# Parting the PSUM ring of stage one: two banks for part-array rounds, two for the first layer

## The chip, the cores and the metric

The kernel runs on one core of a Trainium2 chip. The metric is the device time of one execution in microseconds (us). Before the change it is 1588.79 us, the median of three runs (1582.47 to 1589.11). One execution was profiled, with times, waits and the clock of every engine; the rows below come from it. TensorE is called PE here, VectorE DVE, ScalarE ACT, GpSimd POOL, and SP issues the DMAs.

## The reference

An attention through 32 packed queries for each head is followed by two feed-forward layers. The second of these makes up most of the later half of the kernel; the change lies in everything ahead of it.

```python
def sm_attn(qq, kk, vv):
    s = scale * np.matmul(qq, kk.transpose(0, 1, 3, 2))
    s = s - np.max(s, axis=-1, keepdims=True)
    a = np.exp(s)
    a = a / (np.sum(a, axis=-1, keepdims=True) + 1e-09)
    return np.matmul(a, vv)
p_packed = sm_attn(p, k, v)              # 8 batches, 8 heads, 32 x 64
out = sm_attn(q, p_packed, p_packed)     # 576 x 64 for each head
...
h = x @ w_in                             # first layers: 512 -> 2048 -> 512
g = h * np.cos(h)
x = g @ w_out
h = x @ w2_in
g = h * np.tanh(softplus(h))
return g @ w2_out
```

## The kernel before

**Stage one** does the attention and the first feed-forward layer. Its 4608 tokens are 16 tiles of 288 (two for each batch), and the 2048 hidden channels are 16 groups of 128, so there are 256 steps `n`. The second product of the attention is folded into the layer's weights: `w_unit` multiplies the packed rows `PK` of a batch by `w_in`, and `l1` then multiplies those products (`W1`) by the attention weights `AT` of a token tile. A step has three parts on PE and beside it:

- `l1(n)`: six matmuls of 288 columns (each operand is a high and a low part, three products for each of two halves) into one bank of PSUM.
- the chain `chain_first`, `chain_cos`, `chain_split`, which makes `g = h cos h` of that bank: L793 on ACT, L795 and L796 on DVE, the sine L802 on ACT, the product with `h` L803 on DVE (the last reader of the bank), then the high part L810 on ACT and the low part L813 on POOL.
- `l2(n - 3)`: twelve matmuls of 288 columns, three for each of four banks `acc`.

Between these, `run_bg` and `run_ew` bring the background work of the step, planned in the tables `bg_pe`, `bg_ew` and `bg_ld`. Its PE part consists of small rounds in which a matmul fills only a part of the array (64 rows or 128 by 32 columns), so that several of them can run side by side on different parts:

- `k_unit` (16 of them): `s2_pe` scores packed queries against keys, eight matmuls into two banks (L215); `s4_pe` transposes (L250, L251, the whole array); `s5_pe` multiplies by the values, twenty matmuls into one bank (L276); `s6_pe` transposes once more (L294).
- `q_unit` (16): `s2_pe`, eight matmuls into two banks (L348).
- `w_unit` (40): four matmuls for each batch (L488), so eight into two banks where it serves two batches (24 units), four into one bank where it serves one (16 units).

All of these and `l1` take their bank from `ring()`, one ring of four. The other four banks are the accumulators of `l2`. The same `ring` serves the products of stage two. A float32 matmul of such a round leaves two records in the trace, so a round of eight is shown as x16.

The order on each engine is made when the program is built: a scheduler takes the instruction that is ready by its own timeline, by priorities (`tc.high_priority`) and by orders asked for with `tc.issue_after`. In `w_unit` the other matmuls are asked to follow the first; in the other units nothing keeps the matmuls of a round together.

**Stage two** does the second layer in five blocks of tokens, from about 860 us to the end.

Of the kernel before, what the change touches and what calls it, by code (L numbers as in the profile page):

```python
# [8 lines left out]
F32 = mybir.dt.float32  # L9
# [6 lines left out]
B, H, S, D, NPK = 8, 8, 576, 64, 32  # L16
# [52 lines left out]
HP_W = 400  # L69
K3 = (0, 2, 1, 3, 5, 4, 6)  # L70
# [14 lines left out]
def build(tc, q, k, v, p, w1i, w1o, w2i, w2o, out):  # L85
    nc = tc.nc
    ctx = ExitStack()
    with ctx:
# [10 lines left out]
        def ring():  # L99
            return psum.tile([128, 512], F32, tag="ps", bufs=4, name=nm("ps"))  # L100
# [56 lines left out]

        PK = {}
        lastexp = [None]

        def k_unit(b, g, alloc_v):
# [16 lines left out]
            def vload(i):  # L178
                def f():
# [7 lines left out]
                    else:  # L187
                        nc.sync.dma_start(
                            r[:64, :256].rearrange("p (h d) -> p h d", d=D),
# [20 lines left out]
            def s2_pe():  # L210
                st["s1"] = [ring() for _ in range(2)]
                for l in range(4):
                    h = PERM[par][l]
                    for x in range(2):
                        nc.tensor.matmul(  # L215
                            st["s1"][x][32 * l : 32 * l + 32, :TT].rearrange("p (s a) -> p a s", a=9),
                            st["pp"][64 * x : 64 * x + 64, 32 * h : 32 * h + 32],
                            st["kt"][64 * x : 64 * x + 64, TT * h : TT * h + TT].rearrange("p (a s) -> p a s", s=32),
                            start=True,
                            stop=True,  # L220
                        )
# [23 lines left out]
            def s4_pe():  # L245
                e = st["e"]
                t1, t2 = ring(), ring()
                ev = e[:, :512].rearrange("p (t c) -> p c t", c=4)
                for c in range(4):
                    nc.tensor.transpose(t1[:, 128 * c : 128 * c + 128], ev[:, c], ident)  # L250
                nc.tensor.transpose(t2[:64, :128], e[:, 512:576], ident)  # L251
                st["t"] = (t1, t2)

            def s4_ew():
# [4 lines left out]
                nc.scalar.copy(a5[:64], t2[:64, :128])  # L259
# [6 lines left out]
            def s5_pe():  # L266
                a4, a5 = st["a"]
                ps = ring()
                for c in range(5):
                    n = 128 if c < 4 else 64  # L270
                    a = a4[:, 128 * c : 128 * c + 128] if c < 4 else a5[:64]
                    for l in range(4):
                        h = PERM[par][l]
                        vr = st["vr"][h // 2] if c < 4 else st["vr"][2]
                        o = 256 * (h % 2) + D * c if c < 4 else D * h
                        nc.tensor.matmul(  # L276
                            ps[32 * l : 32 * l + 32, :D],
# [200 lines left out]
        def w_unit(bs, fg, g, ms):  # L478
            st = {}

            def pe():
                for b in bs:
                    st[b] = ring()
# [675 lines left out]
```

## Time and profile before

| what | us |
|---|---|
| median of three runs | 1588.79 |
| the profiled execution, its own time | 1587.78 |
| its span, first to last instruction | 1585.8 |
| PE busy in the span | 1492.7 |
| DVE busy | 1093.4 |
| ACT busy | 895.0 |
| POOL busy | 672.3 |

The span is 1.98 us shorter than the execution's own time, and that execution lies 1.01 us under the median. PE is busy for 94% of the span. Matmuls are pipelined and their ends are modelled, so the time that a group of matmuls takes is best read from start to start: when matmuls of 288 columns follow each other without a wait, they start about 0.13 us apart, though each is shown as 0.29 us long.

### The profile page before, as it was taken

How to read it: one execution, taken by the hardware profiler on the slowest of the kernel's cores; microseconds unless marked ns; L12 is line 12 of the kernel's file. 1: busy time of each engine (PE TensorE's matmuls, PEld its weight loads, DVE VectorE, ACT ScalarE, POOL GpSimd, SP SyncE). 2: the span in 40 equal slices, each digit the busy share in tenths (PEclk: the TensorE clock that was granted, in tenths of full speed). 3: DMA queues.
4: the chain of work that ended last, by engine and by line, in shares of the span. 5: the costliest groups of instructions: out<-in, count | busy, mean ns of one | idle time of the engine just before them, and what ended most of it. 6: DMA issues, size and time to landing. Idle time of an engine off the chain costs nothing.

```text
span 1585.8 us, 28624 instructions
## 1 busy us (share of the span) xinstructions
PE 1492.7 (94%) x9728; PEld 1302.5 (82%) x9728; DVE 1093.4 (69%) x2044; ACT 895.0 (56%) x1844; POOL 672.3 (42%) x682
## 2 busy tenths in 40 slices
PE   3778999999999999998999999999999999999997
PEld 1566778788987898788999888889999899999986
DVE  4885667677766776778764557687567658756656
ACT  3675767677766776766764345435444533543343
POOL 0451346357653665647843025225223521532142
PEclk9889999999999999999999999999999999999999
DMA  9888676557556556543323668788778878777955
GB/s 290 276 214 206 175 186 191 170 146 205 154 158 180 168 163 164 175 123 109 120 68 119 198 197 248 204 231 263 232 214 258 253 213 229 240 215 207 262 150 169
DMA packets 250833, 307.05 MB, mean 194 GB/s; under 512 B 104768, under 2 KB 129856, under 8 KB 250688
## 3 DMA queue, kind: packets, MB, share of 16 engines
q1 hardware_dynamic: 250688, 305.22, 66.6%
q8 instruction: 78, 1.28, 0.3%
q14 instruction: 67, 0.55, 0.1%
HBM read 252.71 MB, written 52.43 MB: 192 GB/s over the span
## 4 chain that ended last, share of the span: by engine, by line
PE 70%; DMA 9%; DVE 7%; ACT 4%; issue 4%; POOL 4%; SPq 1%; DVEq 0%; POOLq 0%; ACTq 0%
PE acc L142 12%; PE acc L143 12%; PE acc L144 12%; PE ps L142 10%; PE ps L143 10%; PE ps L144 10%; PE ps L488 2%; POOL wt L563 2%; DMA raw<-in_moe_w_out_dram 2%; DMA raw<-in_moe_w_in_dram 1%; DVE r L796 1%; DMA kr<-in_k_dram 1%; DVE r L795 1%; DMA kr<-in_q_dram 1%; POOL raw L569 1%
## 5 line engine op out<-in xcount | busy, mean ns | idle before, releaser
L813 POOL TENSOR_TENSOR gh<-r,gh 128x288 fp32r<-128x288 f32 x256 | 216.7, 853 | 286.3 <-ACT gh L810 204.1
L937 POOL TENSOR_TENSOR gh<-t,gh 128x448 fp32r<-128x448 f32 (+1 forms) x120 | 155.2, 1298 | 427.9 <-ACT gh L936 427.9
L143 PE MATMUL acc<-gh,wo 128*128 128x288 f32 x1024 | 301.7, 301 | 1.8 <-POOL gh L813 1.6
L144 PE MATMUL acc<-gh,wo 128*128 128x288 f32 x1024 | 298.2, 298 | 0.0
L142 PE MATMUL acc<-gh,wo 128*128 128x288 f32 x1024 | 276.7, 305 | 6.7 <-ACT gh L810 5.9
L142 PEld LDWEIGHTS acc<-gh,wo 128*128 128x128 f32 x1024 | 182.3, 191 | 41.7 <-issue 16.5
L143 PE MATMUL acc<-gh,T 128*128 128x448 f32 (+1 forms) x560 | 209.6, 374 | 1.3 <-DVE gh L937 1.3
L144 PE MATMUL acc<-gh,T 128*128 128x448 f32 (+1 forms) x560 | 208.9, 374 | 0.0
L143 PE MATMUL ps<-wab,ws 128*128 128x448 f32 (+1 forms) x560 | 208.2, 372 | 0.0
L142 PE MATMUL ps<-wab,ws 128*128 128x448 f32 (+1 forms) x560 | 206.7, 372 | 1.3 <-DMA ws<-wst 1.2
L143 PEld LDWEIGHTS acc<-gh,wo 128*128 128x128 f32 x1024 | 194.1, 190 | 15.8 <-issue 10.1
L144 PE MATMUL ps<-wab,ws 128*128 128x448 f32 (+1 forms) x560 | 206.9, 372 | 0.0
L144 PEld LDWEIGHTS acc<-gh,wo 128*128 128x128 f32 x1024 | 194.2, 190 | 4.1 <-issue 4.0
L937 DVE TENSOR_TENSOR gh<-wo,gh 128x448 fp32r<-128x448 f32 (+1 forms) x160 | 128.8, 810 | 95.4 <-ACT gh L936 94.6
L142 PE MATMUL acc<-gh,T 128*128 128x448 f32 (+1 forms) x560 | 186.5, 375 | 3.2 <-ACT gh L936 3.2
L142 PE MATMUL ps<-aT,wab 128*128 128x288 f32 x512 | 161.1, 315 | 28.2 <-DVE r L803 20.1
L802 ACT ACTIVATE r<-r,halfpi 128x288 f32<-128x288 f32 x256 | 136.2, 535 | 84.4 <-DVE r L796 82.8
L803 DVE TENSOR_TENSOR r<-r,ps 128x288 f32<-128x288 f32 x256 | 114.4, 448 | 69.1 <-ACT r L802 68.1
L143 PE MATMUL ps<-aT,wab 128*128 128x288 f32 x512 | 153.1, 299 | 0.0
L144 PE MATMUL ps<-aT,wab 128*128 128x288 f32 x512 | 152.4, 298 | 0.0
L795 DVE SCALAR_TENSOR_TENSOR r<-ki,ps 128x288 f32<-128x288 int32 x256 | 113.5, 446 | 55.0 <-ACT ki L793 35.7
L793 ACT ACTIVATE ki<-ps,quarter 128x288 int32<-128x288 f32 x256 | 124.0, 495 | 47.5 <-PE ps L144 36.8
(150 smaller groups left out, 2968.5 us busy)
## 6 DMA issues: line engine op xcount, KB each, us to landing
ws<-wst SPq DMA_DIRECT2D x280, 256.0 KB, 3.0
T<-tst SPq DMA_DIRECT2D x280, 256.0 KB, 2.9
kr<-in_k_dram SPq DMA_DIRECT2D x64, 272.0 KB, 5.4
ld<-ws SPq DMA_DIRECT2D x64, 256.0 KB, 3.7
kr<-in_q_dram SPq DMA_DIRECT2D x60, 272.0 KB, 5.3
wst<-wt SPq DMA_DIRECT2D x56, 256.0 KB, 2.7
tst<-wt SPq DMA_DIRECT2D x56, 256.0 KB, 2.2
x2d<-xo SPq DMA_DIRECT2D x64, 144.0 KB, 1.8
```

The costliest lines, as they stand in the source:

```text
L142: nc.tensor.matmul(ps, l0, r0, start=first, stop=False, skip_group_check=more)
L143: nc.tensor.matmul(ps, l0, r1, start=False, stop=False, skip_group_check=more)
L144: nc.tensor.matmul(ps, l1, r0, start=False, stop=last, skip_group_check=more)
L488: return nc.tensor.matmul(st[b][32 * l : 32 * l + 32], PK[(b, g)][r : r + 64, 32 * l : 32 * l + 32], ms[h // 2]["m"][r : r + 64], start=Tr ...
L563: nc.gpsimd.tensor_tensor(lo, src, hi, ALU.subtract)
L569: nc.gpsimd.tensor_tensor(quad(raw, a), quad(raw, b), quad(raw, c), d)
L793: nc.scalar.activation(ki, st["h"], AF.Identity, bias=quarter, scale=1.0 / TWO_PI)
L795: nc.vector.scalar_tensor_tensor(r, ki, -TWO_PI, st["h"], ALU.mult, ALU.add)
L802: nc.scalar.activation(g, g, AF.Sin, bias=halfpi, scale=1.0)
L803: nc.vector.tensor_tensor(g, g, st["h"], ALU.mult)
L813: nc.gpsimd.tensor_tensor(gh[:, 1], st["g"], gh[:, 0], ALU.subtract)
L937: eng.tensor_tensor(hl[:, 1, :n], src, hl[:, 0, :n], ALU.subtract)
```

## The change

- `ring()` is parted. `small()` is a ring of two banks (tag `sm`) for the part-array rounds and the transposes of stage one; `ring()` itself has two banks (tag `ps`).
- `l1` uses the `ps` banks. Where no background PE work is planned in the steps `n-2` to `n+1` (`QUIET`), it takes the two rings in turn. The products of stage two take them in turn always.
- All small rounds go through `rounds`: each is issued after the last matmul of the round before it (`chain`), and its other matmuls follow its first by `issue_after` with a raised priority.
- A round of two banks is led by `hold`, a matmul of the whole array with 16 columns into the first of its two banks. There are 56: 16 for `k_unit`, 16 for `q_unit`, 24 for `w_unit` with two batches.
- The matmuls of a score round are sorted by head, from the last one down. The value product starts with the last 64 keys, which now stand in partitions 64 to 127: their transpose takes columns 448 to 576 of the exponentials, the copy to `a5` and the load of `v` use the upper half.
- The exponential of a `k_unit` (`s3`) is emitted in the step of its maximum (`s2_ew`).

```diff
-        def ring():
-            return psum.tile([128, 512], F32, tag="ps", bufs=4, name=nm("ps"))
+        def small():
+            return psum.tile([128, 512], F32, tag="sm", bufs=2, name=nm("sm"))
+
+        def ring(x=0):
+            return small() if x % 2 else psum.tile([128, 512], F32, tag="ps", bufs=2, name=nm("ps"))
...
+        def hold(ps, src):
+            nc.tensor.matmul(ps[:, :HOLD_N], ident, src[:, :HOLD_N], start=True, stop=True)
...
+        def rounds(banks, src, first, rest):
+            with ExitStack() as es:
+                if chain[0] is not None:
+                    es.enter_context(tc.issue_after(chain[0]))
+                for ps in banks:
+                    hold(ps, src)
+                es.enter_context(tc.high_priority(offset=HP_W if banks else 0))
+                ins = first()
+            with tc.issue_after(getattr(ins, "ins", ins)), tc.high_priority(offset=HP_W):
+                for f in rest:
+                    ins = f()
+            chain[0] = getattr(ins, "ins", ins)
...
-                nc.tensor.transpose(t2[:64, :128], e[:, 512:576], ident)
+                todo.append(lambda: nc.tensor.transpose(t2[:, :128], e[:, 448:576], ident))
...
-                (s2_pe, s2_ew),
-                (None, s3),
+                (s2_pe, lambda: (s2_ew(), s3())),
+                (None, lambda: None),
...
+        small_at = set(bg_pe)
+        turn = [0]
...
-            ps = ring()
+            quiet = not any(n + d in small_at for d in QUIET)
+            if quiet:
+                turn[0] += 1
+            ps = ring(turn[0] if quiet else 0)
...
-                        ps = ring()[:, :n]
+                        turn[0] += 1
+                        ps = ring(turn[0])[:, :n]
```

**How it moves PE's instructions.** In the rows below `ps`, `sm` and `acc` are banks of PSUM, `pk` packed rows, `ld` a loaded piece of `w_in`, `aT` attention weights, `wab` the folded weights, `gh` the hidden layer of a step.

The first place is on PE, at 489 to 492 us of the trace: one `w_unit` of two batches. Before:

```order
L144 MATMUL ps_1227_6292<-aT_1175_6034,wab_1146_5888 128x288
L488 MATMUL ps_1229_6300<-ld_1213_6228,pk_929_4698 32x512 x2
L488 MATMUL ps_1229_6300<-ld_1205_6181,pk_929_4698 32x512 x2
L142 MATMUL acc1_1104_5662<-gh_1221_6270,wo_252_1166 128x288
L143 MATMUL acc1_1104_5662<-gh_1221_6270,wo_252_1166 128x288
L144 MATMUL acc1_1104_5662<-gh_1221_6270,wo_252_1166 128x288
L142 MATMUL acc2_1105_5663<-gh_1221_6270,wo_252_1166 128x288
L488 MATMUL ps_1228_6299<-ld_1213_6228,pk_646_3224 32x512 x2
L488 MATMUL ps_1228_6299<-ld_1205_6181,pk_646_3224 32x512 x2
```

The same unit on PE now:

```order
L149 MATMUL ps_1252_6460<-aT_1175_6065,wab_1146_5918 128x288
L147 MATMUL acc1_1256_6479<-gh_1233_6384,wo_90_436 128x288
L147 MATMUL acc0_1255_6478<-gh_1233_6384,wo_90_436 128x288
L520 MATMUL sm_1229_6334<-ld_1213_6262,pk_929_4724 32x512 x2
L520 MATMUL sm_1228_6333<-ld_1213_6262,pk_646_3239 32x512 x2
L520 MATMUL sm_1229_6334<-ld_1205_6214,pk_929_4724 32x512 x2
L520 MATMUL sm_1228_6333<-ld_1205_6214,pk_646_3239 32x512 x2
L147 MATMUL acc2_1257_6480<-gh_1233_6384,wo_90_436 128x288
```

The two banks were filled one after the other with four matmuls of `l2` between them, and are now filled in one round of eight; its `hold` stands one `l1` and two matmuls of `l2` ahead of it.

The second place is on PE, at 499 to 502 us: the second bank of a `q_unit`'s scores, whose first bank had been filled 2.3 us earlier. Before:

```order
L143 MATMUL acc3_1258_6445<-gh_1245_6402,wo_100_472 128x288
L348 MATMUL ps_1254_6433<-kt_1237_6360,pk_806_4030 32x288
L142 MATMUL ps_1266_6481<-aT_1175_6034,wab_1194_6131 128x288
L143 MATMUL ps_1266_6481<-aT_1175_6034,wab_1194_6131 128x288
L144 MATMUL ps_1266_6481<-aT_1175_6034,wab_1194_6131 128x288
L142 MATMUL ps_1266_6481<-aT_1175_6034,wab_1194_6131 128x288
L143 MATMUL ps_1266_6481<-aT_1175_6034,wab_1194_6131 128x288
L144 MATMUL ps_1266_6481<-aT_1175_6034,wab_1194_6131 128x288
L348 MATMUL ps_1254_6433<-kt_1237_6360,pk_806_4030 32x288 x3
L144 MATMUL acc3_1258_6445<-gh_1245_6402,wo_100_472 128x288
```

The whole round of that `q_unit` on PE now:

```order
L149 MATMUL acc0_1255_6478<-gh_1282_6611,wo_137_629 128x288
L377 MATMUL sm_1254_6468<-kt_1237_6395,pk_806_4054 32x288
L377 MATMUL sm_1253_6467<-kt_1237_6395,pk_646_3239 32x288
L377 MATMUL sm_1254_6468<-kt_1237_6395,pk_806_4054 32x288
L377 MATMUL sm_1253_6467<-kt_1237_6395,pk_646_3239 32x288
L377 MATMUL sm_1254_6468<-kt_1237_6395,pk_806_4054 32x288
L377 MATMUL sm_1253_6467<-kt_1237_6395,pk_646_3239 32x288
L377 MATMUL sm_1254_6468<-kt_1237_6395,pk_806_4054 32x288
L377 MATMUL sm_1253_6467<-kt_1237_6395,pk_646_3239 32x288
L147 MATMUL ps_1300_6687<-aT_1175_6065,wab_1194_6164 128x288
```

Three pieces with an `l1` and matmuls of `l2` between them became one round of eight that takes the two banks by turns.

The third place is on PE, about 300 us: two steps of `l1` while the folded weights of a new pair of batches are being made. Before, `l1` of `ps_815` stands in one piece:

```order
L142 MATMUL ps_815_4071<-aT_666_3324,wab_771_3851 128x288
L143 MATMUL ps_815_4071<-aT_666_3324,wab_771_3851 128x288
L144 MATMUL ps_815_4071<-aT_666_3324,wab_771_3851 128x288
L142 MATMUL ps_815_4071<-aT_666_3324,wab_771_3851 128x288
L143 MATMUL ps_815_4071<-aT_666_3324,wab_771_3851 128x288
L144 MATMUL ps_815_4071<-aT_666_3324,wab_771_3851 128x288
```

Now its first half stands some 50 rows earlier on PE, and here are the second halves of it and of the next step:

```order
L302 MATMUL sm_790_3957<-ld_775_3885,tmp_784_3929 32x64
L147 MATMUL ps_815_4095<-aT_666_3340,wab_771_3874 128x288
L148 MATMUL ps_815_4095<-aT_666_3340,wab_771_3874 128x288
L147 MATMUL ps_821_4130<-aT_666_3340,wab_771_3874 128x288
L148 MATMUL ps_821_4130<-aT_666_3340,wab_771_3874 128x288
L149 MATMUL ps_815_4095<-aT_666_3340,wab_771_3874 128x288
L149 MATMUL ps_821_4130<-aT_666_3340,wab_771_3874 128x288
L323 MATMUL sm_800_4024<-ident_79,pxw_796_4009 128x128
```

Both `ps` banks are open until the second half of the weights is there, and no other step can start in them meanwhile.

## Rows read from the trace of the kernel before

**Rows 1.** Busy time by stretch; columns: stretch, its length, engines, clock, DMA share, GB/s.

```profile
44.00:160.00 116.00, 93.96 (x694) 75.54 (x694) 90.33 (x189) 80.00 (x158) 48.58 (x45) 0.88 0.87 235
160.00:860.00 700.00, 674.05 (x5526) 589.59 (x5525) 500.05 (x1096) 490.94 (x1081) 394.45 (x457) 1.00 0.53 152
860.00:1500.00 640.00, 638.72 (x3029) 567.96 (x3028) 427.00 (x634) 278.41 (x518) 194.20 (x148) 1.00 0.78 230
```

**Rows 2.** Timeline of PE, one whole `w_unit`; columns: start, us, instruction, [idle before].

```profile
482.08 0.29 PE L144 MATMUL acc<-gh,wo 128*128 128x288 f32 x1
482.21 0.29 PE L142 MATMUL acc<-gh,wo 128*128 128x288 f32 x1
482.43 1.09 PE L488 MATMUL ps<-ld,pk 64*32 64x512 f32 x16
483.45 0.40 PE L143 MATMUL acc<-gh,wo 128*128 128x288 f32 x1
483.69 0.29 PE L144 MATMUL acc<-gh,wo 128*128 128x288 f32 x1
```

**Rows 3.** Timeline of PE, half of a `w_unit` that is filled in two pieces.

```profile
489.11 1.06 PE L488 MATMUL ps<-ld,pk 64*32 64x512 f32 x8
490.10 0.40 PE L142 MATMUL acc<-gh,wo 128*128 128x288 f32 x1
```

**Rows 4.** Timeline of PE, key scores: a half round and a whole one.

```profile
474.73 0.69 PE L215 MATMUL ps<-kt,pp 64*32 64x288 f32 x8
475.35 0.40 PE L144 MATMUL acc<-gh,wo 128*128 128x288 f32 x1
...
508.42 0.71 PE L215 MATMUL ps<-kt,pp 64*32 64x288 f32 x16
509.07 0.40 PE L142 MATMUL ps<-aT,wab 128*128 128x288 f32 x1
```

**Rows 5.** Timeline of PE, value products: one in two pieces, then a whole one.

```profile
491.82 0.65 PE L276 MATMUL ps<-ld,tmp 128*32 128x64 f32 x32
...
492.64 0.40 PE L142 MATMUL ps<-aT,wab 128*128 128x288 f32 x1
...
493.62 0.30 PE L276 MATMUL ps<-ld,a 64*32 64x64 f32 x2
493.85 0.40 PE L143 MATMUL acc<-gh,wo 128*128 128x288 f32 x1
...
525.36 0.65 PE L276 MATMUL ps<-ld,tmp 128*32 128x64 f32 x32
...
526.19 0.40 PE L143 MATMUL acc<-gh,wo 128*128 128x288 f32 x1
```

**Rows 6.** Timeline of PE, four transposes with the identity as the moving or stationary side.

```profile
485.25 0.63 PE L250 MATMUL ps<-ident,tmp 128*128 128x128 f32 x4
485.64 0.38 PE L142 MATMUL acc<-gh,wo 128*128 128x288 f32 x1
```

**Rows 7.** Timeline of PE and DVE: two steps of `l1`, and L803 of each.

```profile
506.45 0.29 PE L144 MATMUL ps<-aT,wab 128*128 128x288 f32 x1
509.42 0.45 DVE L803 TENSOR_TENSOR r<-r,ps 128x288 f32<-128x288 f32 x1 [0.66 <-ACT r L802]
509.83 0.30 PE L144 MATMUL ps<-aT,wab 128*128 128x288 f32 x1
516.47 0.46 DVE L803 TENSOR_TENSOR r<-r,ps 128x288 f32<-128x288 f32 x1 [1.40 <-ACT r L802]
```

**Rows 8.** Waits of the whole span; columns: us in total, times, longest.

```profile
PE ps L142 <- DVE r L803: 20.1, 19, 5.9
...
PE acc L142 <- ACT gh L810: 5.9, 4, 3.1
```

**Rows 9.** Timeline of PE, the first steps of stage one.

```profile
56.35 0.61 PE L142 MATMUL ps<-aT,wab 128*128 128x288 f32 x1 [5.93 <-DVE r L803]
...
87.75 1.93 PE L488 MATMUL ps<-wab,pk 64*32 64x512 f32 x8 [4.35 <-DVE wab L438]
```

More of the change, by code (lines that the diff above doesn't have):

```diff
@@ L69 @@
 HP_W = 400
+HOLD_N = 16
+QUIET = (-2, -1, 0, 1)
 K3 = (0, 2, 1, 3, 5, 4, 6)
@@ L210, in s2_pe, with head @@
             def s2_pe():
-                st["s1"] = [ring() for _ in range(2)]
-                for l in range(4):
+                st["s1"] = [small() for _ in range(2)]
+                def head(x, l):
                     h = PERM[par][l]
[L214 to L221, printed above, removed]
+                    return nc.tensor.matmul(
+                        st["s1"][x][32 * l : 32 * l + 32, :TT].rearrange("p (s a) -> p a s", a=9),
+                        st["pp"][64 * x : 64 * x + 64, 32 * h : 32 * h + 32],
+                        st["kt"][64 * x : 64 * x + 64, TT * h : TT * h + TT].rearrange("p (a s) -> p a s", s=32),
+                        start=True,
+                        stop=True,
+                    )
+                todo = [lambda x=x, l=l: head(x, l) for x, l in sorted(((x, l) for x in range(2) for l in range(4)), key=lambda y: (-PERM[par][y[1]], -y[0]))]
+                rounds(st["s1"][:1], st["kt"][:, 576:], todo[0], todo[1:])
             def s2_ew():
@@ L246, in s4_pe @@
                 e = st["e"]
-                t1, t2 = ring(), ring()
+                t1, t2 = small(), small()
                 ev = e[:, :512].rearrange("p (t c) -> p c t", c=4)
-                for c in range(4):
-                    nc.tensor.transpose(t1[:, 128 * c : 128 * c + 128], ev[:, c], ident)
-                nc.tensor.transpose(t2[:64, :128], e[:, 512:576], ident)
+                todo = [lambda c=c: nc.tensor.transpose(t1[:, 128 * c : 128 * c + 128], ev[:, c], ident) for c in range(4)]
+                todo.append(lambda: nc.tensor.transpose(t2[:, :128], e[:, 448:576], ident))
+                rounds((), None, todo[0], todo[1:])
                 st["t"] = (t1, t2)
@@ L292, in s6_pe @@
             def s6_pe():
-                ps = ring()
-                nc.tensor.transpose(ps[:, :128], st["xw"].rearrange("p a d -> p (a d)"), ident)
+                ps = small()
+                rounds((), None, lambda: nc.tensor.transpose(ps[:, :128], st["xw"].rearrange("p a d -> p (a d)"), ident), [])
                 st["xt"] = ps
@@ L482, in pe @@
                 for b in bs:
-                    st[b] = ring()
+                    st[b] = small()
                 def head(b, l):
@@ L496, in pe @@
                 todo = sorted(((b, l) for b in bs for l in range(4)), key=lambda x: (-(PERM[x[0] % 2][x[1]] // 2), -x[0]))
[L497 to L500 removed]
+                rounds([st[b] for b in bs[:-1]], ms[1]["m"], lambda: head(*todo[0]), [lambda x=x: head(*x) for x in todo[1:]])
             def ew():
```

61 lines of the change are left out of this document (30 added, 31 removed).

## The prediction

> **What bounds the kernel now.** I read the busy time by stretch first [rows 1]. From 860 us on, PE is busy for 638.72 of 640 us: stage two is a stream of matmuls without gaps, and its ring keeps four banks in the same turn, so I leave it as it is. Between 160 and 860 us PE is busy for 674.05 of 700 us and DVE for 500.05: stage one is bound by PE too, with 26.0 us of gaps. Only its first stretch, 44 to 160 us, is different: PE lacks 22.0 of 116 us, its clock is at 0.88, and DVE with 90.33 us is nearly as full. There PE waits for the first chains and for converted weights [rows 9]. So a microsecond taken off PE's work after 160 us is worth about one, and before it little. Next I read the small rounds on PE's timeline from start to start [rows 2 to 5], because that is the work that the change regroups, and then what PE waits for [rows 8], because that is what a shorter ring could add to.
>
> **What leaving a round costs.** Full matmuls start 0.13 us apart (482.08, 482.21). Into a round it is 0.22 us, and the first full matmul after it is followed by the next in 0.24 us [rows 2]. Each piece of a round thus pays 0.09 + 0.11 = 0.20 us for the two changes, beside its body.
>
> - *Folded weights.* A whole unit's body is 483.45 - 482.43 = 1.02 us [rows 2], half a unit's 0.99 us [rows 3]: the second bank rides along for nothing. A split unit costs 2 x 1.19 - 1.22 = 1.16 us more. In the order of before 10 of the 24 units of two batches are split, now none: -11.6 us.
> - *Key scores.* Half a round takes 0.62 us, a whole one 0.65 us [rows 4]; a further piece costs 2 x 0.82 - 0.85 = 0.79 us. 16 units had 22 pieces, now 16: -4.7 us.
> - *Query scores.* They have the same shape on PE, so I take the same 0.79 us. 16 units had 32 pieces, now 16: -12.6 us.
> - *Value products.* The larger piece takes 0.82 us (491.82 to 492.64), its rest of two records 0.23 us, a whole round 0.83 us [rows 5]: a split costs 0.82 + 0.23 + 0.40 - 1.03 = 0.42 us. 28 pieces became 17: -4.6 us.
>
> Together -33.5 us of PE work.
>
> **What the holds cost.** No row shows a float32 product of the whole array. The nearest is the transposes, four in 0.39 us, 0.10 us each [rows 6]. A float32 matmul leaves two records, so I take 2 x 0.10 = 0.20 us: 56 x 0.20 = 11.2 us. It is at least 0, where PE would have waited for the bank anyway, and at most about 0.30 us (two full matmuls of 0.13 us and a little), 16.8 us. Net PE work: -22.3 us. Of the pieces six fall before 160 us (4 x 0.79 + 2 x 0.42 = 4.0 us, against 8 holds of 1.6 us); I count that 2.4 us as nothing, since PE is not the bound there. That leaves **-20 us**.
>
> A hold also is an added wait: PE takes its instructions in order, and behind a hold that waits for the readers of its bank stand matmuls of `l1` and `l2`, for which the chain on ACT and DVE waits. Before, the first matmul of the round waited in the same way, only a few matmuls later, so I give the hold's own wait no price apart from those below.
>
> **What goes with no price.** The transpose of the last keys moves as many columns as before, the load of `v` and the copy to `a5` move the same bytes to other partitions on the same queues, and the first-half order of the value product has the same matmuls. The earlier exponential moves two activations by a step on ACT, which is busy for 490.94 of 700 us [rows 1]; if that cover were gone it would show as a later L802.
>
> **What the shorter ring costs.** An `l1` may start when L803 two uses back in its ring has read the bank. That chain took 3.1 us from the end of `l1` (506.74) to the end of L803 (509.87) in one step, and 6.8 us (510.13 to 516.93) in the next, where L803 waited for ACT [rows 7]. Against that stands the PE work between the end of an `l1` and the next use of its bank. I summed it over the order of either kernel, 0.13 us for a full matmul and the pieces above for the rounds: its median falls from 6.6 to 5.7 us, and it is under 5 us in 22 of 252 cases before, in 52 now. All of these were paid for in the 20.1 us of [rows 8], 19 waits of 1.06 us on average.
>
> The second layer loses distance too. `l1` led `l2` by 4.9 steps on average and now by 4.5, and the order shows where the low part of `gh` is late: there the four high products stand ahead of the others. This is so in 67 of 256 steps before, and in 90 now. The third place of the order shows one cause: the last folded weights of the first two pairs come two to three steps later, behind the other rounds, and hold both `ps` banks open.
>
> I price this by the idle time of stage one, 22.0 + 26.0 = 48 us [rows 1], scaled with that count: 48 x 90 / 67 = 64.5, so **+16.5 us**. Its lower end is 0: the short chain of 3.1 us fits all but some nine of the 252 distances. Its upper end goes by the waits themselves: 30 more short distances x 1.06 us = +32 us, and 23 more late steps at the 1.5 us of the four waits for L810 [rows 8] = +34 us, if both come in full. I take the value near the lower third because each wait gives the chains in flight the same time, so that not every late one costs again.
>
> **Sum.** -20 + 16.5 = -3.5 us on the profiled execution's 1587.78 us, 1584.3 us; that execution lies 1.0 us under the median, so about **1585 us** beside 1588.79.
>
> **A rule that speaks against the change.** In the half round of [rows 3] four matmuls, two on the upper and two on the lower 64 rows of the array, write the same bank in 0.99 us, and the whole round takes 1.02 us. The Trainium skill, "TensorEngine Tiling (Array Packing)", Restrictions and Gotchas, says that different row tiles cannot access the same PSUM bank simultaneously. By that rule whole rounds would run one after the other and their 11.6 us for the folded weights would be lost; the trace does not agree, and I go by the rows.
>
> **Rivals.**
> - *The chains fit.* The new order was made for the new ring, and waits stay as they are: -20 us, 1569 us; with free holds 1557 us. For it: L803 mostly ends in time, and only 19 of 252 uses waited. Against it: the slow chain of 6.8 us is longer than the new median distance.
> - *The short ring starves PE.* The mechanism is one: `l1` waits for L803 two uses back, behind it `l2` runs dry. With 30 more waits of 1.06 us it is -20 + 32 = +12 us, 1601 us; with the late `l2` as well +46 us, 1635 us. It decides from 20 / 30 = 0.67 us for each of the 30 shorter distances on. For it: steps of 6 to 7 us as in [rows 7], and at 56 us a first wait of 5.93 us for L803 that already came with four banks [rows 9].
> - *Whole rounds gain nothing.* Should a round of eight run in two halves after all (the rule above), the sum becomes -3.5 + 11.6 = +8 us, 1597 us. [Rows 2] speak against it.
>
> **How the numbers follow.** A measurement of this kernel can tell about 0.5% from no change, 8 us: under 1581 is faster, over 1597 slower. My forecast covers 1577 to 1597 us (waits +8 to +28 us) with a chance of 0.50, of which 0.10 lies under 1581, 0.37 within, 0.03 above. The chains fit: 0.24, faster. Starving: 0.24, slower. No gain from whole rounds: 0.02, slower. So faster 0.34, same 0.37, slower 0.29. The range leaves out about a tenth at each end: below 1566 (free holds, no added waits) and above 1606 (both waits in good part).
>
> **What would show it.** In the profile after, every query, key and two-batch weight round should be whole (x16) with bodies of 0.65 and 1.02 us, and a hold of about 0.2 us; between 160 us and the end of stage one PE's busy time should fall by about 20 us, while its gaps grow by some 16 us, put down to L803 and L810. If the waits for L803 stay near 20 us in total, the first rival holds; if they pass 50 us, the second. If holds take over 0.3 us, or a whole round over 1.3 us, my prices were wrong.

## The result

The changed kernel takes 1608.69 us (median of 4 runs, 1605.53 to 1614.67) against 1586.42 us for the kernel before on the same chip: the ratio is 1.0147, with a 95% interval of 1.0107 to 1.0186. It is slower by some 22 us. The time lies 24 us above the forecast of 1585 us, and above the range of 1566 to 1606 us. The profiled execution took 1605.53 us with a span of 1603.8 us.

The busy time by stretch of the kernel after answers to [rows 1] (stretch, its length, PE, weight loads, DVE, ACT, POOL, clock, DMA share, GB/s):

```profile
44.00:160.00 116.00, 89.59 (x621) 75.59 (x618) 87.60 (x173) 74.84 (x148) 49.25 (x45) 0.81 0.82 225
160.00:860.00 700.00, 643.64 (x5517) 580.35 (x5516) 492.10 (x1088) 492.19 (x1070) 383.25 (x446) 0.99 0.54 152
882.00:1522.00 640.00, 639.38 (x3072) 575.20 (x3071) 431.91 (x641) 279.27 (x524) 199.26 (x150) 1.00 0.78 233
```

Stage two is as full as it was. In the same 700 us of stage one PE is busy for 30.4 us less, and its gaps have grown from 26.0 to 56.4 us; the first stretch has the lower clock as well, 0.81 in place of 0.88.

The rounds themselves came out as forecast. The timeline of PE in the kernel after shows a hold and two whole rounds (start, us, instruction); they answer to [rows 2, 4]:

```profile
461.02 0.29 PE L149 MATMUL acc<-gh,wo 128*128 128x288 f32 x1
461.16 0.29 PE L164 MATMUL sm<-kt,ident 128*128 128x16 f32 x2
461.30 0.51 PE L147 MATMUL acc<-gh,wo 128*128 128x288 f32 x2
...
463.72 0.71 PE L377 MATMUL sm<-kt,pk 64*32 64x288 f32 x16
464.37 0.40 PE L149 MATMUL acc<-gh,wo 128*128 128x288 f32 x1
...
491.22 0.29 PE L164 MATMUL sm<-ld,ident 128*128 128x16 f32 x2
491.44 1.09 PE L520 MATMUL sm<-ld,pk 64*32 64x512 f32 x16
492.46 0.40 PE L147 MATMUL ps<-aT,wab 128*128 128x288 f32 x1
```

A hold takes 0.14 us from its start to the next (461.16 to 461.30). A whole query round takes 0.65 us and whole folded weights 1.02 us (491.44 to 492.46). The Trainium skill, "TensorEngine Tiling (Array Packing)", Restrictions and Gotchas, says that different row tiles cannot access the same PSUM bank simultaneously; eight matmuls on both row halves into two banks in 1.02 us don't agree with it, as the prediction held.

PE's waits between 44 and 860 us in the kernel after (total us, times, longest) answer to [rows 8]:

```profile
PE ps L147 <- DVE r L837: 50.3, 42, 4.7
PE acc L148 <- POOL gh L847: 6.7, 10, 1.8
...
PE sm L164 <- ACT tmp L261: 3.8, 3, 2.6
PE sm L275 <- ACT tmp L261: 2.6, 1, 2.6
```

L837 is the product with `h` that was L803. The wait of `l1` for it was 20.1 us in 19 waits and is 50.3 us in 42. The prediction had named 50 us as the sign of its second rival, the starving ring.

**One account for all kernels.** From 44 us to the start of the last `l2` step (857.4 us before, 882.1 after) I split each profile three ways. *Gaps* are the stretch less PE's busy time. *Low clock* is busy time multiplied by what the granted clock lacked of 1.00, summed over windows of 1 us. *Work* is the rest. The whole stretch of the kernel before and, behind it, of the kernel after:

```profile
44.00:857.40 813.40, 765.41 (x6200) 662.70 (x6200) 589.91 (x1282) 570.14 (x1236) 443.04 (x501) 0.98 0.58 164
```

```profile
44.00:882.10 838.10, 755.32 (x6302) 678.04 (x6299) 591.29 (x1285) 577.74 (x1240) 443.34 (x503) 0.96 0.56 159
```

Gaps are 813.40 - 765.41 = 48.0 us before and 82.8 us after, the low clock costs 14.9 and 25.8 us, and work is 750.5 and 729.5 us. So stage one ends later by -21.0 + 34.8 + 10.9 = +24.7 us. In the profiled executions 8 us of this are hidden again, since stage two took 708.5 us after and 716.4 us before; the last section returns to that. *Work* is what is left over: it also takes in short waits that lie under the shown length of a matmul (0.29 us, at starts 0.13 us apart), so a few microseconds of it mean little.

### The profile page after: what moved, and what is told of

It reads as the page before. It is cut to its first block, busy times and chain, and to the rows that moved or that the text cites. A ratio compares the mean times of both kernels' runs of the same rounds, so it can differ in the third digit from the quotient of the medians.

```text
span 1603.8 us, 28880 instructions
## 1 busy us (share of the span) xinstructions
PE 1476.9 (92%) x9840; PEld 1319.1 (82%) x9840; DVE 1094.1 (68%) x2044; ACT 899.5 (56%) x1846; POOL 673.0 (42%) x682
## 4 chain that ended last, share of the span: by engine, by line
PE 62%; DVE 10%; DMA 9%; ACT 8%; issue 5%; POOL 4%; SPq 1%; DVEq 0%; ACTq 0%; POOLq 0%
PE acc L147 11%; PE acc L148 11%; PE acc L149 11%; PE ps L147 6%; PE ps L148 5%; PE ps L149 5%; PE sm L147 4%; PE sm L148 4%; PE sm L149 4%; DVE r L830 2%; DMA raw<-in_moe_w_in_dram 2%; POOL wt L592 2%; ACT r L836 2%; DVE r L829 2%; DVE r L837 1%
## 5 line engine op out<-in xcount | busy, mean ns | idle before, releaser
L148 PE MATMUL acc<-gh,wo 128*128 128x288 f32 x1024 | 301.8, 303 | 6.8 <-POOL gh L847 6.7
L149 PE MATMUL acc<-gh,wo 128*128 128x288 f32 x1024 | 298.2, 300 | 0.0
L147 PE MATMUL acc<-gh,wo 128*128 128x288 f32 x1024 | 260.6, 303 | 2.7 <-ACT gh L844 1.4
L147 PEld LDWEIGHTS acc<-gh,wo 128*128 128x128 f32 x1024 | 180.0, 193 | 14.9 <-ACT gh L844 3.5
L971 DVE TENSOR_TENSOR gh<-wo,gh 128x448 fp32r<-128x448 f32 (+1 forms) x160 | 129.0, 812 | 86.3 <-ACT gh L970 85.6
L147 PE MATMUL acc<-gh,T 128*128 128x448 f32 (+1 forms) x560 | 184.1, 374 | 3.3 <-ACT gh L970 3.2
L147 PE MATMUL ps<-aT,wab 128*128 128x288 f32 x422 | 136.7, 325 | 51.8 <-DVE r L837 50.3
L147 PEld LDWEIGHTS ps<-aT,wab 128*128 128x128 f32 x422 | 82.7, 196 | 81.6 <-DVE r L837 67.3
L837 DVE TENSOR_TENSOR r<-r,ps 128x288 f32<-128x288 f32 x211 | 94.3, 449 | 74.6 <-ACT r L836 73.9
L830 DVE TENSOR_SCALAR r<-r 128x288 f32<-128x288 f32 x256 | 131.1, 517 | 4.6
L148 PE MATMUL ps<-aT,wab 128*128 128x288 f32 x422 | 129.0, 306 | 1.2 <-POOL aT L423 1.2
L970 ACT CAST gh<-wo 128x448 fp32r<-128x448 f32 (+1 forms) x160 | 92.1, 578 | 66.6 <-PE acc L149 65.8
L844 ACT CAST gh<-r 128x288 fp32r<-128x288 f32 x256 | 108.6, 430 | 37.0 <-DVE r L837 24.5
L149 PE MATMUL ps<-aT,wab 128*128 128x288 f32 x422 | 128.4, 306 | 0.0
L827 ACT ACTIVATE ki<-ps,quarter 128x288 int32<-128x288 f32 x211 | 103.5, 498 | 44.1 <-PE ps L149 39.7
```

The lines of the kernel that those rows point to most:

```text
L147: nc.tensor.matmul(ps, l0, r0, start=first, stop=False, skip_group_check=more)
L148: nc.tensor.matmul(ps, l0, r1, start=False, stop=False, skip_group_check=more)
L149: nc.tensor.matmul(ps, l1, r0, start=False, stop=last, skip_group_check=more)
L827: nc.scalar.activation(ki, st["h"], AF.Identity, bias=quarter, scale=1.0 / TWO_PI)
L830: (nc.gpsimd if n % C_MOD in C_POOL else nc.vector).tensor_scalar(r, r, 1.570796, -4.712388, ALU.min, ALU.max)
L837: nc.vector.tensor_tensor(g, g, st["h"], ALU.mult)
```

## The experiments

**Theory A** said that the ring of two makes `l1` wait; **theory B** that the fixed order of the rounds and the holds do it. The first four runs give back the one ring of four, take the holds away, or make `l1`'s ring shorter and longer.

**One ring of four again** (`e_shared`): whole rounds, holds and order are kept.

```diff
-            return psum.tile([128, 512], F32, tag="sm", bufs=2, name=nm("sm"))
+            return psum.tile([128, 512], F32, tag="ps", bufs=4, name=nm("sm"))
...
-            return small() if x % 2 else psum.tile([128, 512], F32, tag="ps", bufs=2, name=nm("ps"))
+            return psum.tile([128, 512], F32, tag="ps", bufs=4, name=nm("ps"))
```

> The changed kernel with its ring of four given back: l1, the small rounds and the transposes all take the four banks in turn again; holds, whole rounds and their fixed order stay. Theory A (the parted ring costs the time: l1 waits for the product with h two uses back): the waits of PE for that product fall from 50 us to about 25 us or less, and the whole rounds keep their saving, so the kernel comes out 15 to 25 us under the kernel before, 1562 to 1572 us. Theory B (the fixed order of the rounds and the holds cost the time, not the banks): the waits stay and the time stays near 1605 us.

1582.97 us, ratio to before 0.9986 (0.9967 to 1.0005): no difference from before, and 26 us faster than the change. Parting the ring costs that much, but theory A had also promised that the work saved would then show. It didn't: work fell by 19.8 us, and gaps and low clock rose by 18.5 us. Theory B's 1605 us falls.

**No holds** (`e_nohold`): the ring stays parted, and the rounds are split again.

```diff
-                for ps in banks:
-                    hold(ps, src)
```

> The changed kernel without its 56 holds; the parted ring and the fixed order of the rounds stay. In the order on PE the rounds fall apart again (56 pieces of folded weights, 29 of key scores, 26 of query scores, against 37, 16 and 16 with holds). Theory A: the parted ring stays, so the added waits stay, and the split rounds come back: 20 us over the changed kernel, about 1625 us. Theory B (PE stands at the holds, in order, and everything behind them waits): without them the waits fall and the time falls to 1595 us or less.

1595.22 us, 1.0076 (1.0050 to 1.0102): 13 us faster than the change although PE has 33.9 us more work (763.4 us). Gaps are 50.8 us, hardly more than before:

```profile
44.00:870.80 826.80, 775.98 (x6197) 661.83 (x6194) 588.54 (x1284) 577.81 (x1239) 441.15 (x502) 0.98 0.57 161
```

Theory A's 1625 us falls, and theory B's bound of 1595 us is missed by 0.2 us only: the parted ring with split rounds barely waits. Neither theory holds for both runs.

**`l1` never in the rounds' banks, or always by turns** (`e_never`, `e_both`):

```diff
-QUIET = (-2, -1, 0, 1)
+QUIET = tuple(range(-300, 300))
```

```diff
-QUIET = (-2, -1, 0, 1)
+QUIET = ()
```

> The changed kernel in which l1 never takes the banks of the rounds: two banks for it throughout stage one. In the order of PE 134 of 252 distances between an l1 and the next use of its bank are under 5 us of PE work (52 in the changed kernel), and l1 leads l2 by 3.0 steps on average (4.5). Theory A: the waits for the product with h grow with that count, by 60 us or more, over 1660 us. Theory B: the rounds and their order are the same, so the time moves by less than 15 us from 1609.

> The changed kernel in which l1 always takes the two rings in turn, so that it has four banks, two of them shared with the small rounds, which keep only two. In the order of PE l1 leads l2 by 5.1 steps (4.5 in the changed kernel, 4.9 before), but the lowest tenth of the distances is 2.2 us (4.5). Theory A: with more lead the waits of l2 fall and those for a bank of a round rise; 1590 to 1605 us, under the changed kernel. Theory B: l1 in the banks of the rounds delays the rounds further, over 1615 us.

1646.91 us (1.0396, 1.0367 to 1.0425) and 1708.46 us (1.0781, 1.0742 to 1.0820). With two banks alone the kernel loses 38 us more than with the change, which neither theory gave (over 1660 us, or within 15 us of 1609 us). The ring's length costs time, then, but not by the wait that theory A named: `l1` waits 41.7 us for its bank, less than the 50.3 us of the change, and `l2` waits 21.9 us for `gh`, in place of 8.1.

```profile
PE ps L147 <- DVE r L837: 41.7, 42, 3.7
PE acc L147 <- ACT gh L844: 14.4, 13, 2.9
PE acc L148 <- POOL gh L847: 7.5, 9, 2.5
```

```profile
44.00:923.20 879.20, 783.98 (x6326) 689.91 (x6323) 597.25 (x1281) 585.54 (x1240) 442.30 (x502) 0.95 0.55 152
```

Gaps are 95.2 us and the low clock costs 34.9 us; why the account's work rises to 749.1 us, with the rounds as whole as in the change, isn't known. `l1` in the rounds' banks at all times is far worse: rounds (without their holds) then wait 54.0 us for L837, and full matmuls 33.6 us for background work. Theory A had put it at 1590 to 1605 us, theory B only at over 1615 us. The table of quiet steps is the best of the three, but by the groups of instructions of the kernel after it gives `l1` a second pair of banks seldom (each step has two records of L147):

```profile
L147 PE MATMUL ps<-aT,wab 128*128 128x288 f32 x373 | 118.4, 318 | 39.3 <-DVE r L837 38.2 <-ACT wab L536 1.0
...
L147 PE MATMUL sm<-aT,wab 128*128 128x288 f32 x88 | 27.0, 306 | 2.5 <-ACT pk L328 2.5
```

From 160 us on 44 steps of some 230 stand in `sm`.

**Is it simply that PE has less to do?** If ACT and DVE bound stage one, any work taken off PE would come back as waits (theory C). Against it stands theory D, that whole rounds cost because they keep two banks at once. Two runs leave work out and touch nothing else: `e_less` in the kernel before, `e_nohless` in `e_nohold`, the parted ring without holds (there `skip=n % 4 == 2`).

```diff
-        def mm3(ps, l0, l1, r0, r1, first, last, more=False):
+        def mm3(ps, l0, l1, r0, r1, first, last, more=False, skip=False):
...
-            nc.tensor.matmul(ps, l1, r0, start=False, stop=last, skip_group_check=more)
+            if not skip:
+                nc.tensor.matmul(ps, l1, r0, start=False, stop=last, skip_group_check=more)
...
-                mm3(acc[t][dc][:, :TT], w[:, 0, o : o + 128], w[:, 1, o : o + 128], gh[:, 0], gh[:, 1], s == 0, s == NF - 1)
+                mm3(
+                    acc[t][dc][:, :TT], w[:, 0, o : o + 128], w[:, 1, o : o + 128], gh[:, 0], gh[:, 1], s == 0, s == NF - 1, skip=n % 6 == 3 and s < NF - 1
+                )
```

> The kernel before, with PE work simply left out and nothing else changed: in 37 of the 256 steps (n mod 6 = 3, not the last of a tile) l2 leaves out its third product, the low part of the weights, in all four banks. So part of the computation is missing. 148 full matmuls of 0.13 us are gone, and with small shifts of the order PE's work in stage one is 734.3 - 27.3 = 707.0 us, as in the changed kernel (707.9). Theory C, the chain bounds: whatever PE saves in stage one comes back as gaps and as a lower clock, because a step needs its time on ACT and DVE; then stage one ends 0 to 8 us earlier and the time is 1577 to 1585 us. Theory D, the reserved banks: the waits of the kernel with whole rounds in a ring of four come from the two banks that a held round keeps at once, and other savings arrive; then the time is 1584 - 25 = 1559 us (1555 to 1565).

1561.68 us, 0.9852 (0.9818 to 0.9887): in this run the work left out arrives in full, and theory C fails for the ring of four. Stage one ends 23.9 us earlier, of which 17.4 us are work and 7.0 us the low clock; in a second sample, below, only about half of it arrives. Its stretch has 789.50 - 741.03 = 48.5 us of gaps, as before, and `l1`'s wait for its bank is as before:

```profile
44.00:833.50 789.50, 741.03 (x6057) 638.08 (x6054) 587.46 (x1283) 567.86 (x1238) 443.29 (x501) 0.99 0.60 169
```

```profile
PE ps L142 <- DVE r L804: 21.7, 21, 5.7
```

> The parted ring without holds, with PE work left out as well: in every fourth step (n mod 4 = 2, 64 steps) l2 leaves out its third product in all four banks, so part of the computation is missing. PE's work in stage one is 737.5 - 30.1 = 707.4 us, as much as in the changed kernel (707.9), but the rounds are split as without holds. It tells whether the changed kernel loses its 25 us to the short ring when PE has less to do, or to the holds. Theory C: the short ring's chains bound, PE waits in place of the work left out, and the time is near the changed kernel's: 1590 to 1608 us. Theory D: without holds no bank is reserved, the 30 us arrive nearly in full: 1562 to 1575 us.

1583.68 us, 0.9998 (0.9974 to 1.0022), where 1595.22 us were needed with 37.5 us more work: of what was left out two thirds came back. In the parted ring theory C is nearer, then. It has slack for a PE that is busy with split rounds, and none for one that is faster. Gaps are 67.0 us:

```profile
44.00:858.50 814.50, 747.54 (x5940) 633.38 (x5937) 593.90 (x1282) 577.42 (x1239) 442.85 (x502) 0.97 0.58 164
```

**Parts alone.** `e_bw` adds to the kernel before only the holds ahead of the 24 two-batch weight rounds; `e_shnohold` has everything but the holds and the parted ring (the edits of `e_shared` and `e_nohold` together).

```diff
+                for b in bs[:-1]:
+                    nc.tensor.matmul(st[b][:, :16], ident, ms[1]["m"][:, :16], start=True, stop=True)
                 ins = head(*todo[0])
```

> The kernel before with one part alone: a hold ahead of each round of folded weights that serves two batches (24 holds), in the ring of four; the score rounds, the value products and their order are as before. The split rounds of this kind go from 11 more pieces to none: PE's work is 734.3 - 11.2 = 723.1 us. Theory C: nearly all of it comes back as waits, 1580 to 1586 us. Theory D: 24 of 56 holds cost 24/56 of the 18.5 us that whole rounds lost in the ring of four, 8 us, so 1584 - 11 + 8 = 1581 us (1577 to 1585). The run weighs this part alone rather than telling the two apart.

> The changed kernel with one ring of four for all and without the holds: what is left of the change is the fixed order of the rounds, their sorted matmuls, the value products in one piece, and the earlier exponential. PE's work is 731.6 us, 2.7 us less than before, and l1 leads l2 by 5.4 steps on average (4.9 before). Theory C and theory D both say that little happens: 1578 to 1586 us; under D, which prices reserved banks alone, 1581 us, under C 1583 us. If it is slower than 1592 us, the fixed order costs something by itself, which neither theory says.

1584.90 us (0.9995, 0.9973 to 1.0017) and 1582.82 us (0.9975, 0.9949 to 1.0000). Whole weight rounds alone take 11.1 us of work away and bring 7.7 us of gaps and 7.2 us of low clock. The fixed order, the sorted matmuls and the earlier exponential cost nothing that can be measured.

**Does the time between hold and round set the price?** `e_bwhi` and `e_bwlo` are `e_bw` with each hold at a raised and at a lowered priority, so that 36.9 and 9.2 us of PE work stand between holds and rounds, in place of 19.3 us (the diff is that of `e_bwhi`; `e_bwlo` has -300).

```diff
-                    nc.tensor.matmul(st[b][:, :16], ident, ms[1]["m"][:, :16], start=True, stop=True)
+                    with tc.high_priority(offset=300):
+                        nc.tensor.matmul(st[b][:, :16], ident, ms[1]["m"][:, :16], start=True, stop=True)
```

> The kernel before with its 24 holds ahead of the two-batch weight rounds, each hold issued earlier (raised priority): between the hold and its round stand 36.9 us of PE work in the order, summed over all 24, in place of 19.3 us. The pieces are the same and PE's work too (721.9 and 723.1 us). Theory D, now put as reserved time: what a whole round costs goes with the time for which its first bank lies between hold and round. The 14 us of added loss with 19.3 us become 14 x 36.9 / 19.3 = 27 us, the time is 1585 + 13 = 1598 us (1592 to 1603). Rival E: a whole round costs a fixed amount, because both its banks are read by ACT and DVE at the same time afterwards; then the hold's place is of no weight and the time stays at 1581 to 1588 us.

> The same with each hold issued later (lowered priority): 9.2 us of PE work between the holds and their rounds in place of 19.3 us, the rounds as whole as before and PE's work 724.4 us. Theory D: 14 us of loss become 14 x 9.2 / 19.3 = 7 us, the time is 1585 - 7 + 1 = 1579 us (1575 to 1583). Rival E, a fixed cost of each whole round: 1583 to 1588 us.

1585.63 us (1.0004, 0.9984 to 1.0023) and 1589.56 us (1.0025, 1.0005 to 1.0046). Gaps are 54.0, 55.7 and 55.8 us with 36.9, 19.3 and 9.2 us reserved. The price doesn't follow the reserved time, and this form of theory D falls: a whole round costs what it costs wherever its hold stands. That is rival E in its number (`e_bwlo` lies 1.6 us above its range); its reason, that ACT and DVE then read both banks at once, no run has tested.

**A fifth bank** (`e_b5`, `e_a5`): the products of the fourth accumulator go into the bank of the third, so that this part of the result is left out, and the bank that comes free is given to the ring: in `e_a5` to every third step of `l1` that doesn't use `sm`, in `e_b5` to every fifth user of the one ring. The diff is that of `e_a5`.

```diff
-            return [psum.tile([128, 512], F32, tag=f"acc{j}", bufs=1, name=nm(f"acc{j}")) for j in range(4)]
+            a = [psum.tile([128, 512], F32, tag=f"acc{j}", bufs=1, name=nm(f"acc{j}")) for j in range(3 if five[0] else 4)]
+            return a + [a[2]] if five[0] else a
...
+            if five[0] and x % 2 == 0:
+                use[0] += 1
+                if use[0] % 3 == 0:
+                    return psum.tile([128, 512], F32, tag="acc3", bufs=1, name=nm("ps"))
...
```

> The changed kernel with a fifth bank: in stage one the fourth accumulator's products are added into the third accumulator's bank, so the output is wrong there, while PE, ACT, DVE and the DMAs have the same work; the bank that comes free goes to l1, whose own ring is three long, and the rounds keep two. Holds, whole rounds and PE's work (707.5 us) are as in the changed kernel, the distance from l1 to the next use of its bank rises from 5.8 to 7.5 us (median). If the ring of two is what costs its 29 us, the time is 1608.7 - 29 = 1580 us or somewhat less (1565 to 1584). If the loss comes from the holds and the fixed order alone, it stays over 1598 us.

> The kernel before with the same fifth bank (the fourth accumulator's products added into the third's, so the output is wrong there), as the measure for the run beside it: one ring of five, rounds split as they fall. PE's work is 729.0 us (734.3 with four). Of the 63 us of gaps and low clock a part goes: 1584 - 5 - 5 = 1574 us (1566 to 1582). If the parted ring of three and two with whole rounds is the faster of the two, the change's idea holds where banks suffice.

1617.56 us (1.0204, 1.0172 to 1.0236) and 1599.98 us (1.0091, 1.0064 to 1.0119). Both are slower than with four banks, which no theory said, so they decide nothing about the ring of two, although `e_a5` stays over the 1598 us that were to speak for holds and order alone. From the end of `l1` to the end of the product with `h`, steps 64 to 191 took 4.7 us in the median before and 6.2 us in `e_b5`; 5.1 us after and 7.2 us in `e_a5`. `l1` still waited 40.3 us for its bank in `e_a5`: the longer ring met a longer chain. I have not found out why the chain grew.

**The four corners again.** By now each combination of ring and rounds, at nearly the same PE work, had been seen in one order only. Four more runs take each in another order: other steps are left out (`n % 6 == 0` in `e_less2`, `n % 4 == 0` in `e_nohless2`), the exponential goes back to its old step (`e_shs3`, made from `e_shared`), the holds get a lowered priority (`e_alo`, made from the change). Theory F: ring and rounds are each a cause. Rival G: the accidents of the order are.

> Second sample of the corner 'ring of four, rounds split, less PE work': the kernel before, with l2's third product left out in other steps (n mod 6 = 0), so part of the computation is missing. PE's work is 713.0 us in its order. Theory F: the parted ring costs about 30 us of gaps and low clock, whole rounds about 25 us, whatever the accidents of the order; the four corners at nearly equal PE work then keep their ranks. From 44 us to the end of stage one, gaps and low clock lost 56 us in the first sample of this corner: expected 50 to 64 us, and 1584 - 21 = 1563 us (1558 to 1569). Rival G, accidents of the order: every edit reshuffles ACT's and DVE's order, and the corners differ by luck; then this one may lose 70 us or more, 1575 to 1585 us.

> Second sample of the corner 'ring of four, rounds whole': the changed kernel with one ring of four for all and the exponential of a k_unit back in its old step. Holds and pieces are as in the first sample, PE's work is 710.9 us. Theory F: gaps and low clock lose 73 to 90 us from 44 us to the end of stage one (81 in the first sample), 1577 to 1589 us. Rival G: it may as well lose 56 to 65 us as other kernels in the ring of four, 1560 to 1572 us.

> Second sample of the corner 'parted ring, rounds split, less PE work': no holds, and l2's third product left out in other steps (n mod 4 = 0), so part of the computation is missing. PE's work is 709.8 us. Theory F: gaps and low clock lose 80 to 97 us (89 in the first sample), 1584 + 2 = 1586 us (1580 to 1592). Rival G: 56 to 70 us or over 105 us, outside 1575 to 1597 us.

> Second sample of the corner 'parted ring, rounds whole': the changed kernel with its 56 holds issued later (lowered priority). Between hold and round stand 51 us of PE work in the order, summed; PE's work is 708.3 us. Theory F: gaps and low clock lose 100 to 117 us (109 in the first sample), 1600 to 1616 us. Rival G: 90 us or less, under 1592 us.

| ring, rounds | kernel | time | work | gaps | low clock |
|---|---|---|---|---|---|
| four, split | `e_less` / `e_less2` | 1561.68 / 1574.28 | 733.1 / 731.2 | 48.5 / 52.1 | 7.9 / 19.5 |
| four, whole | `e_shared` / `e_shs3` | 1582.97 / 1579.83 | 730.7 / 725.6 | 64.2 / 62.1 | 17.2 / 23.5 |
| parted, split | `e_nohless` / `e_nohless2` | 1583.68 / 1589.13 | 725.9 / 729.2 | 67.0 / 69.7 | 21.5 / 18.1 |
| parted, whole | after / `e_alo` | 1608.69 / 1613.27 | 729.5 / 727.2 | 82.8 / 85.4 | 25.8 / 29.1 |

(us; the ratios to before of the four second samples are 0.9939, 0.9974, 1.0031 and 1.0174, intervals 0.9918 to 0.9959, 0.9952 to 0.9996, 1.0006 to 1.0057 and 1.0127 to 1.0221.) The gaps of the table follow from the stretches, here of `e_alo`, `e_shared`, `e_less2`, `e_shs3` and `e_nohless2` in this order; the others stand above.

```profile
44.00:885.70 841.70, 756.31 (x6306) 682.68 (x6299) 584.68 (x1285) 580.23 (x1240) 443.44 (x503) 0.96 0.56 158
```

```profile
44.00:856.10 812.10, 747.94 (x6306) 673.02 (x6307) 594.74 (x1282) 569.09 (x1234) 443.22 (x502) 0.98 0.58 164
```

```profile
44.00:846.80 802.80, 750.70 (x6032) 645.55 (x6029) 588.54 (x1283) 570.15 (x1238) 442.31 (x502) 0.97 0.59 166
```

```profile
44.00:855.20 811.20, 749.11 (x6306) 675.55 (x6307) 590.52 (x1282) 573.65 (x1238) 443.90 (x502) 0.97 0.59 164
```

```profile
44.00:861.00 817.00, 747.33 (x5940) 632.31 (x5938) 581.15 (x1283) 579.90 (x1239) 443.88 (x502) 0.97 0.58 163
```

Two samples of a corner differ by 2 to 4 us of gaps, and the other corners lie 13 to 34 us above the first: theory F stands for the gaps. With the mean of each corner, whole rounds add 63.1 - 50.3 = 12.8 us in the ring of four, the parted ring adds 68.3 - 50.3 = 18.0 us, and both together 84.1 - 50.3 = 33.8 us, about their sum of 30.8. The low clock is the part that rival G has right: in one corner it cost 7.9 and 19.5 us.

The ranges set beforehand were for the sum of gaps and low clock. By it three of the four second samples came as theory F said (85.6, 87.8 and 114.5 us). `e_less2` did not: with 71.6 us it has the "70 us or more" of rival G, and its time lies between the two theories' ranges. Of 19.3 us of work left out about 10 us arrived there. The corners keep their ranks by the sum too.

The wait of `l1` for its bank doesn't add up in this way. It is 21.7 and 25.5 us in the first corner, 27.1 and 25.1 us with whole rounds, 29.6 and 35.8 us with the parted ring, and 50.3 and 47.0 us with both: most of its rise needs both at once.

The Trainium skill, "Perfetto Trace Analysis", Optimizing Tensor Performance, advises that independent matmul groups rotate through different PSUM banks, so that evacuation overlaps the next group; the 18.0 us of the parted ring, in which each kind of group has two banks to rotate through and not four, agree with it.

## Why the prediction was wrong

**PE's work was right.** The prediction said -22.3 us, and by the account it fell by 21.0 us. The holds were cheaper than their 0.20 us (0.14 us, 7.8 us for all 56), and whole rounds and pieces came as listed.

**The step that failed is "What the shorter ring costs".** It gave the waits +16.5 us and the clock nothing; gaps and low clock together rose by 34.8 + 10.9 = 45.7 us. As a price of the ring alone 16.5 us is near the 18.0 us of gaps that the corners show, but by luck: it was scaled from the late steps of `l2`, and `l2` hardly waited more. By what PE waited for between 44 us and the end of stage one:

- `l1` for its bank: from 20.1 to 50.3 us, +30.2 us. The upper end in the prediction was +32 us. It took the lower third, because a wait gives the other chains time. They didn't use it: 42 waits cost 1.20 us each, 19 had cost 1.06.
- `l2` for `gh`: from 7.5 to 8.1 us, where up to +34 us stood in the prediction. The late low part of `gh`, counted from the order, was worth nothing.
- Rounds and holds for their own operands and for the readers of rounds before them: from 8.3 to 17.4 us, +9.1 us. This had been given no price: "I give the hold's own wait no price apart from those below". The holds aren't needed for it, though: with split rounds and no holds the parted ring has 19.2 us of the same waits (`e_nohless`).
- The rest, of the same kinds as before, fell by some 5 us.

The count of distances under 5 us, on which the upper end rested, says little about the wait: the change has 52 of them and 50.3 us of that wait, `e_nohless` about 55 and 29.6 us, `e_nohless2` about 64 and 35.8 us. The count knows the work that PE has between two uses, but not when the chain begins.

**Two things had no term at all.** One is that whole rounds cost waits by themselves: 12.8 us of gaps in the ring of four, 15.8 us in the parted one. The other is the clock. In the timeline of the kernel after, a hold waits for the exponential that read the bank's last scores, then comes a whole round, then an `l1` that waits for its bank:

```profile
535.92 0.29 PE L149 MATMUL acc<-gh,wo 128*128 128x288 f32 x1
538.79 0.40 PE L164 MATMUL sm<-ld,ident 128*128 128x16 f32 x2 [2.58 <-ACT tmp L261]
539.27 1.88 PE L520 MATMUL sm<-ld,pk 64*32 64x512 f32 x16
542.18 0.61 PE L147 MATMUL ps<-aT,wab 128*128 128x288 f32 x1 [1.03 <-DVE r L837]
542.59 0.44 PE L148 MATMUL ps<-aT,wab 128*128 128x288 f32 x1
542.83 0.44 PE L149 MATMUL ps<-aT,wab 128*128 128x288 f32 x1
...
546.93 0.29 PE L149 MATMUL acc<-gh,wo 128*128 128x288 f32 x1
547.06 0.29 PE L148 MATMUL acc<-gh,wo 128*128 128x288 f32 x1
```

The same place by windows of 1 us (columns as in the stretches above):

```profile
538.00:539.00 1.00, 0.21 (x2) 0.21 (x2) 0.55 (x4) 0.85 (x3) 0.00 (x0) 1.00 0.82 198
539.00:540.00 1.00, 0.91 (x11) 0.27 (x17) 0.65 (x4) 0.98 (x4) 0.00 (x0) 0.72 1.09 268
540.00:541.00 1.00, 1.00 (x16) 0.00 (x0) 0.58 (x1) 1.00 (x1) 0.00 (x0) 0.50 1.04 205
...
545.00:546.00 1.00, 1.00 (x6) 1.00 (x6) 0.78 (x2) 0.63 (x2) 1.00 (x2) 0.50 1.18 356
546.00:547.00 1.00, 1.00 (x9) 1.00 (x9) 0.76 (x3) 0.63 (x3) 1.00 (x2) 0.87 0.81 262
```

After the wait of 2.58 us the granted clock falls to 0.50, 1.2 GHz, and full matmuls start 0.24 us apart (542.59 to 542.83) until it is back at 1.00 and they start 0.13 us apart. In this place the lower level cost 2.9 us by the account, more than the wait ahead of it. After 160 us the kernel before has two such falls and the changed one four.

**What stays open.** Why a whole round costs waits isn't settled. It doesn't depend on how long its first bank is reserved. In the ring of four the waits of the rounds for their operands grew with whole rounds in both pairs of samples (7.2 to 11.3 us from `e_less` to `e_shared`, 12.0 to 19.3 us from `e_less2` to `e_shs3`, holds included); `l1`'s wait for its bank grew in the first pair alone. In the parted ring it is the other way: the operands' waits stay at 17 to 19 us, and `l1`'s wait grows. That a round of two banks can only start when both are free and all eight operands are there, and so starts later than its first half did, fits the ring of four but was only argued. Why the chain grew with a fifth bank is open too.

**The rivals.** "The short ring starves PE" (1601 to 1635 us, chance 0.24) came true in time and sign, with half of its mechanism: the ring alone explains 18.0 of 33.8 us of gaps, and `l2` did not run dry. The prediction had left about a tenth above 1606 us, while most of this rival's own range, with its chance of 0.24, lies there: the upper end of the range was too low by its own numbers. "Whole rounds gain nothing" was right in its effect on the time and wrong in its mechanism, as each round ran whole in 1.02 us.

No version gains much. The fastest with the whole computation is `e_shs3` at 0.9974 of before (0.9952 to 0.9996), some 4 us, and `e_shnohold` with split rounds is as fast.

## What to carry to other kernels

Work that PE saves is worth its time only if the waits stay as they are. In the ring of four, left-out products shortened the kernel by 24 us in one run and by 10 us in another, for 17 to 19 us of work; of the 20 us saved by grouping rounds over two banks hardly anything arrived, as gaps and a lower clock took their place. Before PSUM banks are set aside for one kind of work, ask whether the chain that frees the others still fits when PE is faster; a parted ring that hides its waits behind a slow PE shows them as soon as PE gains. Price a wait of PE together with the lower clock that can follow it (here 2.9 us after one of 2.58 us), and price an added wait near its upper bound unless a row shows that the chains catch up.

## What the runs showed beyond this

- **A full-array float32 matmul of 16 columns costs 0.14 us** from start to start, as much as a full one of 288 columns in this kernel (0.13 us), and leaves two records where that one leaves one.
- **The cost of the lower clock isn't told by the gaps.** Two kernels of the same corner, which leave out nearly the same work in different steps, lost 7.9 and 19.5 us to it with 48.5 and 52.1 us of gaps; their times differ by 12.6 us.
- **Stage two differs between profiles.** From the start of its first to that of its last matmul it took 716.4 us in the profile before, 708.5 us after, and 714.2, 707.8 and 708.3 us in `e_bw`, `e_bwhi` and `e_bwlo`, whose edit lies in stage one. The runs of the kernel before spread from 1574 to 1595 us. The cause isn't known; it is why the kernels here are compared by medians of several runs and by stage one of their profiles.
